# Sixteen interleaved groups of eight rows: another row order in the DRAM copy of streamed weights

## The chip, the cores and the metric

The kernel runs on one core of one Trainium2 chip. The metric is the time of one execution on the device in microseconds (us), as the median of several runs. An execution counts as slow when it is over 1.5% above the fastest of the same kernel, and ratios use fast executions only. Below, before and after name the kernel without and with the change.

The engines have short names in the profiles: PE does the matmuls (PEld its weight loads), DVE, ACT and POOL (also called GpSimd) the work on vectors, and SP here only issues DMA transfers. SBUF is the on-chip memory; the kernel's tiles there have 128 partitions, and each row of a weight chunk goes to one of them.

## The reference

The reference computes two independent things and puts them side by side. Part A is a long convolution by FFT. Part B is a recurrent attention over 64 segments of 32 tokens, in which each segment's memory is the output of the one before, so the segments run one after another:

```python
def _B_ref(x, mem0, Wq, Wk, Wv, Wo, seg_len):
    ...                                   # S = 2048, Dm = 1024, H = 32, Dh = 128, M = 8
    mem = mem0
    for s in range(n_seg):                # 64 segments
        xs = x[:, s * seg_len:(s + 1) * seg_len, :].copy()
        h = jnp.concatenate([mem, xs], axis=1)
        q = jnp.einsum('btd,dhe->bhte', h, Wq)      # k and v in the same way
        ...                               # masked softmax attention
        o = jnp.einsum('bhte,hed->btd', o, Wo)
        mem = o[:, :M, :].copy()
        outs.append(o[:, M:, :])
    ...
```

The four weight matrices of part B take 32 MB in bf16, and every segment needs all of them.

## The kernel before

The weights are cut into 64 chunks of 128 rows by 2048 bf16 columns (512 KB, 4 KB a row). Of these 43 stay in SBUF for good. The other 21 are streamed: before the loop they are copied into a DRAM tensor `WS`, one contiguous 512 KB block for each, and in every segment they are loaded again into a ring of six buffers. (One of them is kept aside after the first segment, which leaves 20 loads a segment and 1281 in all.)

```python
PITCH = 2048
...
    def stream_src(ch):
        return WS[ring_order.index(ch), :, 0:2048]
...
    WS = dram.tile([len(ring_order), 128, PITCH], BF, name="WS")
    for ch in ring_order:
        if ch[0] == 3:                                   # chunks of Wo: DRAM to DRAM
            nc.gpsimd.dma_start(dst_view(stream_src(ch), ch), dram_chunk(ch))
...
                    nc.sync.dma_start(t[:], dram_chunk(ch))          # chunks of Wq, Wk, Wv pass
                    if ch in streamed:                               # through SBUF (tile pw)
                        nc.gpsimd.dma_start(stream_src(ch), t[:])
...
    ring = ctx.enter_context(tc.tile_pool(name="b_ring", bufs=RING))  # RING = 6
    def fetch():
        if loads:
            s, ch = loads.pop(0)
            live[s, ch] = t = ring.tile([128, 2048], BF, tag="wring", name="wring")
            nc.sync.dma_start(t[:], stream_src(ch))                   # the load of this study
...
    def done(ch):                        # called after the last matmul that reads the chunk
        if ch in streamed:
            del live[now[0], ch]
            if now[0] == 0 or ch != order_s[KEPT_SLOT]:
                fetch()
```

## Time and profile before

| | before |
|---|---|
| median time | 2397.64 us (2394.31 to 2403.53, 3 runs) |
| first ring load issued | 568 us after the span's start |
| from the first ring packet to the last | 1819 us |
| DMA share and rate in the loop | 0.99, 381 GB/s |

The page of the profiled execution of before. The rows named PEclk, DMA and GB/s divide the span into 40 equal slices; in the first two a digit is a share in tenths (9 is 90% or more), the third is the rate. The last line is a DMA queue: packets, MB, share of the time of 16 engines.

```profile
span 2404.6 us, 76750 instructions
PE 1773.3 (74%) x33620; PEld 893.8 (37%) x33620; DVE 753.8 (31%) x2331; ACT 639.8 (27%) x1143; POOL 367.0 (15%) x1019
...
PEclk8899669996899999999989999999999999989999
DMA  7886985659999999999999999999999999999997
GB/s 280 305 283 206 376 275 140 183 156 387 401 357 393 370 394 369 400 365 399 380 383 379 375 400 376 393 369 402 384 383 375 388 371 397 375 396 385 388 384 288
...
q1 hardware_dynamic: 278120, 767.72, 84.1%
```

From about the tenth slice on the DMA engines are full and nothing else is. The same for the loop alone, in the table by stretches (the last three numbers of its row are granted PE clock, DMA share, GB/s):

```profile
core 0: us, PE busy (x) PEld busy (x) DVE busy (x) ACT busy (x) POOL busy (x), PEclk, DMA share, GB/s
571.00:2404.00 1833.00, 1439.97 (x32000) 748.53 (x32000) 498.40 (x1872) 435.45 (x833) 267.71 (x889) 0.93 0.99 381
```

A share of 0.99 with PE busy for 1440 of 1833 us means that the 16 DMA engines set the pace. The chain of work that ended last, as shares of the span, says the same: the ring load is its largest part.

```profile
DMA 55%; PE 28%; issue 6%; DVE 6%; ACT 2%; POOL 1%; SPq 0%; ACTq 0%; POOLq 0%; DVEq 0%
DMA wring<-WS 47%; PE acc L708 9%; PE yacc L796 5%; PE kb_ps L541 5%; PE tail_acc L657 3%; PE vb_ps L554 2%; DMA X_sb<-in_B_x_dram 1%; DMA SK<-s_sb 1%; DMA pw<-in_B_Wv_dram 1%; ACT s_sb L234 1%; DMA Wearly<-in_B_Wk_dram 1%; PE tps L723 1%; 
```

The costliest group, PE on streamed chunks (busy us, mean ns of one, then idle time before it and what ended it), PE's own waits for the ring (total us, times, longest us), and the line of the ring loads among the DMA issues (count, size, median us from issue to landing):

```profile
L708 PE MATMUL acc<-wring,rec 128*32 128x512 bf16 x4096 | 419.4, 414 | 166.0 <-DMA wring<-WS 131.9
```

```profile
PE acc L708 <- DMA wring<-WS: 131.9, 234, 2.6
...
PE yacc L796 <- DMA wring<-WS: 46.4, 129, 1.7
PE tps L628 <- DMA wring<-WS: 42.2, 3, 41.2
```

```profile
wring<-WS SPq DMA_DIRECT2D x1281, 512.0 KB, 7.3
```

PE waits little for the ring, only 132 + 46 + 42 us, although the DMA sets the pace: six loads run ahead.

One more reading comes from the trace's records of single DMA packets. A ring load moves as 128 packets of 4 KB, as many as it has rows, and 1281 loads make 163,968 of them. They take 161 ns in the median, 168 ns in the mean (160 and 169 over all 4 KB packets of that queue). There are 4-byte packets as well. The SP queue (q1) has 24,524, and 1527 x 16 + 6 x 15 + 2 x 1 = 24,524: 16 for each load, except for six of 15 rows and two of one row. I read this number as that of the DMA engines that take part in a load. The trace does not name a packet's engine, so this is a reading; it fits that 16 is also the number of ring packets under way for the largest part of the time (49%).

### The profile page before, as it was taken

The numbers are of one execution on the slowest core, as the hardware profiler recorded it, in microseconds if no ns is written. First come the engines' busy times: TensorE is split into PE (matmuls) and PEld (weight loads), VectorE is DVE, ScalarE is ACT, GpSimd is POOL, SyncE is SP. The second block draws the span as 40 slices with busy tenths as digits, with TensorE's granted clock in tenths as the row PEclk, the third lists the DMA queues.
The fourth block names the chain that finished last, engine by engine and source line by source line (L and its number), as shares of the span: only waits on it lengthen the run. The fifth ranks groups of instructions, "written<-read, shape, count | busy, mean of one in ns | idle before, by whom it ended". The sixth has DMA issues, their size and how long they took to land.

```text
span 2404.6 us, 76750 instructions
## 1 busy us (share of the span) xinstructions
PE 1773.3 (74%) x33620; PEld 893.8 (37%) x33620; DVE 753.8 (31%) x2331; ACT 639.8 (27%) x1143; POOL 367.0 (15%) x1019
## 2 busy tenths in 40 slices
PE   2655359773777787777877878787777778787776
PEld 1221134331333434343444434343434343444433
DVE  5978322111222222322222222322222223222222
ACT  6966011111222222222222222222222222222222
POOL 5034100000111111111111111111111111111111
PEclk8899669996899999999989999999999999989999
DMA  7886985659999999999999999999999999999997
GB/s 280 305 283 206 376 275 140 183 156 387 401 357 393 370 394 369 400 365 399 380 383 379 375 400 376 393 369 402 384 383 375 388 371 397 375 396 385 388 384 288
DMA packets 308617, 842.07 MB, mean 350 GB/s; under 512 B 83676, under 2 KB 91900, under 8 KB 308279
## 3 DMA queue, kind: packets, MB, share of 16 engines
q1 hardware_dynamic: 278120, 767.72, 84.1%
q0 software_dynamic: 20048, 45.76, 5.6%
q10 hardware_dynamic: 10112, 23.68, 3.0%
q8 instruction: 263, 4.31, 0.7%
q14 instruction: 74, 0.61, 0.1%
HBM read 777.14 MB, written 62.39 MB: 349 GB/s over the span
## 4 chain that ended last, share of the span: by engine, by line
DMA 55%; PE 28%; issue 6%; DVE 6%; ACT 2%; POOL 1%; SPq 0%; ACTq 0%; POOLq 0%; DVEq 0%
DMA wring<-WS 47%; PE acc L708 9%; PE yacc L796 5%; PE kb_ps L541 5%; PE tail_acc L657 3%; PE vb_ps L554 2%; DMA X_sb<-in_B_x_dram 1%; DMA SK<-s_sb 1%; DMA pw<-in_B_Wv_dram 1%; ACT s_sb L234 1%; DMA Wearly<-in_B_Wk_dram 1%; PE tps L723 1%; DMA Wlate<-in_B_Wo_dram 1%; POOL Yre L344 1%; DVE wring L592 1%
## 5 line engine op out<-in xcount | busy, mean ns | idle before, releaser
L708 PE MATMUL acc<-wring,rec 128*32 128x512 bf16 x4096 | 419.4, 414 | 166.0 <-DMA wring<-WS 131.9
L708 PEld LDWEIGHTS <-rec 128*32 128x32 bf16 x12288 | 325.2, 100 | 529.7 <-issue 273.1
L717 ACT CAST qkv_sb<-acc 128x512 bf16<-128x512 f32 x384 | 225.1, 586 | 823.8 <-PE acc L708 775.4
L708 PE MATMUL acc<-Wearly,rec 128*32 128x512 bf16 x4608 | 385.7, 428 | 4.7 <-DVE YB L669 4.7
L796 PEld LDWEIGHTS <-OT 128*32 128x32 bf16 x8192 | 228.4, 101 | 206.0 <-issue 145.3
L796 PE MATMUL yacc<-Wlate,OT 128*32 128x256 bf16 x5632 | 257.4, 290 | 55.3 <-issue 55.2
L708 PE MATMUL acc<-Wlate,rec 128*32 128x512 bf16 x3584 | 276.4, 380 | 0.0
L796 PE MATMUL yacc<-wring,OT 128*32 128x256 bf16 x2560 | 143.8, 288 | 69.2 <-DMA wring<-WS 46.4
L815 DVE COPY KT<-tps 128x512 bf16<-128x512 bf16 x64 | 27.2, 425 | 398.4 <-PE tps L723 398.4
L685 POOL COPY KT<-rec 128x128 bf16<-128x128 bf16 x128 | 38.8, 303 | 664.3 <-DVE wring L592 519.1
L629 DVE COPY rec<-tps 128x64 bf16<-128x64 bf16 x64 | 12.3, 192 | 373.3 <-PE tps L628 363.9
L864 POOL DMA_DIRECT2D out_dram<-Y x64 | 46.0, 719 | 509.0 <-ACT Y L859 484.0
L782 ACT CAST OT<-OTp 128x512 bf16<-128x512 f32 x128 | 75.0, 586 | 164.4 <-PE OTp L773 161.1
L859 ACT CAST Y<-yacc 128x256 bf16<-128x256 f32 x64 | 23.8, 372 | 299.9 <-PE yacc L796 299.9
L723 PE MATMUL tps<-ident,qkv_sb 128*128 128x128 bf16 x1024 | 101.2, 221 | 1.9 <-DVE tps L592 1.9
L723 PEld LDWEIGHTS <-qkv_sb 128*128 128x128 bf16 x1024 | 58.8, 97 | 112.0 <-issue 84.9
L622 POOL DMA_DIRECT2D rec<-REC x64 | 37.4, 584 | 385.7 <-issue 181.7
L786 DVE CAST OTB<-OTp 128x128 bf16<-128x128 f32 x128 | 34.7, 271 | 182.8 <-ACT OT L782 182.8
L592 DVE TENSOR_SCALAR wring<-OTp 128x768 int32<-128x768 int32 x63 | 60.3, 958 | 93.7 <-PE acc L708 53.1
L692 POOL COPY QBm<-rec 128x32 bf16<-128x32 bf16 x512 | 84.6, 213 | 0.0
L541 PE MATMUL kb_ps<-XBT,Wearly 128*128 128x512 bf16 x288 | 81.8, 384 | 0.0
L818 DVE COPY QT<-tps 128x512 bf16<-128x512 bf16 x64 | 27.2, 425 | 160.5 <-PE tps L723 160.5
(201 smaller groups left out, 2233.6 us busy)
## 6 DMA issues: line engine op xcount, KB each, us to landing
wring<-WS SPq DMA_DIRECT2D x1281, 512.0 KB, 7.3
rec<-REC POOLq DMA_DIRECT2D x64, 192.0 KB, 6.3
SK<-s_sb SPq DMA_DIRECT2D x16, 512.0 KB, 4.8
SU<-s_sb SPq DMA_DIRECT2D x16, 512.0 KB, 3.6
Kg<-SK ACTq DMA_DIRECT2D x32, 256.0 KB, 4.2
Ug<-SU SPq DMA_DIRECT2D x32, 256.0 KB, 4.6
WS<-pw POOLq DMA_DIRECT2D x16, 512.0 KB, 6.8
REC<-stage SPq DMA_DIRECT2D x4, 2048.0 KB, 13.0
```

Of the source, the lines that this page charges most:

```text
L541: nc.tensor.matmul(ps[:], lhsT=ws[kc][:, hl * 128:(hl + 1) * 128], rhs=XBT[:, kc].rearrange("p s t -> p (s t)"), start=(kc == 0), stop=(kc ...
L554: nc.tensor.matmul(ps[:], lhsT=XBT[:, kc, 16 * tb:16 * tb + 16, :].rearrange("p s t -> p (s t)"), rhs=ws[kc][:, c * 512:(c + 1) * 512], st ...
L592: nc.vector.tensor_scalar(out=dst, in0=src, scalar1=0, scalar2=None, op0=ALU.bitwise_or)
L657: nc.tensor.matmul(self.acc[32 * dq:32 * dq + 32, 0:256], lhsT=self.OTB[:, c, 4 * g + i, :], rhs=w[:, o:o + 256], start=first, stop=not se ...
L685: nc.gpsimd.tensor_copy(KT[:, :, :, 32:40], KBs[:, 128 * g:128 * g + 128].rearrange("p (c i t) -> p i c t", c=4, i=4))
L692: nc.gpsimd.tensor_copy(q[:, :, 40 * i:40 * i + 8], QBs[:, 128 * g:128 * g + 128].rearrange("p (c i t) -> p c i t", c=4, i=4)[:, :, i, :])
L708: nc.tensor.matmul(self.acc[32 * c:32 * c + 32, :], lhsT=hT[:, kc, :], rhs=w[:, c * 512:(c + 1) * 512], start=(kc == 0), stop=(kc == 7), t ...
L717: nc.scalar.copy(sb[:], self.acc[:])
L723: nc.tensor.transpose(tp[:, i * 128:(i + 1) * 128], sb[:, i * 128:(i + 1) * 128], ident[:])
L782: nc.scalar.copy(OT[:], o_view(g)[:, :, :, 0:32])
L796: nc.tensor.matmul(yacc[32 * dq:32 * dq + 32, 0:256], lhsT=OT[:, c, i, :], rhs=w[:, hh * 1024 + dq * 256:hh * 1024 + (dq + 1) * 256], star ...
L864: nc.gpsimd.dma_start(bass.AP(outb.tensor, outb.offset + SEG * s * 2048, [[256, 4], [2048, 32], [1, 256]]), Y[:])
```

## The change

The rows of each chunk in `WS` are stored in another order: row `16 hi + lo` of the chunk goes to place `8 lo + hi`, with `hi` from 0 to 7 and `lo` from 0 to 15. The load reads them back through the same view, so the tile in SBUF, and every instruction after it, is as before. The likely intent was to have the DMA engines read neighbouring rows of the memory at the same moment instead of rows far apart.

```diff
     def stream_src(ch):
-        return WS[ring_order.index(ch), :, 0:2048]
+        return WS[ring_order.index(ch), :, 0:2048].rearrange("(lo hi) c -> hi lo c", hi=8)
...
     for ch in ring_order:
         if ch[0] == 3:
-            nc.gpsimd.dma_start(dst_view(stream_src(ch), ch), dram_chunk(ch))
+            for hh in range(2):
+                nc.gpsimd.dma_start(stream_src(ch)[:, :, hh * 1024:(hh + 1) * 1024],
+                                    dram_chunk(ch)[:, hh, :].rearrange("(hi lo) d -> hi lo d", hi=8))
```

In the built program the ring load has the same count, bytes and place as before. Only its DRAM side is now a pattern of two levels, 8 groups of 16 rows; below this is written [8][16], and the one of before [128].

## The prediction

> **What bounds the kernel now.** From 571 us to the end the kernel is a loop of 64 segments, about 28.6 us each, bound by the DMA engines: the table by stretches gives it a DMA share of 0.99 at 381 GB/s, PE busy 1440 of 1833 us. The largest entry of the chain of waits is DMA wring<-WS, 47%. The DMA issues list 1281 such loads of 512 KB, 20 a segment, or 164,000 packets of 4 KB. In the trace one takes 160 ns (median; mean 169), so the ring alone fills 1281 x 8 x 169 ns = 1730 us on each of 16 engines; the loop's other traffic is about 90 us per engine.
>
> **What the change does.** Bytes, packets and arithmetic stay; the permutation is written and undone consistently. In the built program the loop's one difference is the shape of the load: its DRAM side is [8][16] rows of 4 KB instead of [128], against 128 SBUF partitions. The copies into WS (five become ten halves, sixteen keep their size) get the same shape, in the first 571 us and mostly off the critical path: 0 to 20 us.
>
> **Why this matters.** [...] the SP queue's 24,524 of them are exactly 1527 loads x 16 + six 15-row loads x 15 + two one-row loads; the ACT queue's 1088 are 66 x 16 + four 8-row loads x 8. None of its DMAs shows it for [8][16].
>
> **Cost.** On 8 engines a load puts 16 packets on each: 1281 x 16 x 160 to 169 ns = 3280 to 3460 us, plus 90, plus 571: 3940 to 4120 us, all on the critical path. It may be worse. [...] The trace hints at such a cost: around 48.5 to 52 us, where 112-row loads run, 2 KB packets take about 128 ns, against 84 in 128-row loads. So I go above the clean sum.
>
> **Prediction.** 4300 us, 80% range 3850 to 5700. Faster by over 2%: 0.03; within 2%: 0.07; slower by over 2%: 0.90.
>
> **What would show each step.** (1) Half the engines: the SP queue's packets fall by 8 x 1281 = 10,248, from 278,120 to about 267,870; the loop's DMA share falls to about 0.5, its rate to about 200 GB/s or less. (2) Clean halving: 4 KB packets stay at 160 to 170 ns[...]. (3) PE's waits for wring<-WS grow from under 300 us to well over 1500. (4) The time before the loop stays within 30 us of 571. (5) Issue to landing of a ring load, 7.3 us now, at least doubles.
>
> **What would make it wrong.** If [8][16] still goes over all 16 engines (the packet count stays), the time stays near 2400 us[...]. If reading rows 32 KB apart eased or hurt the memory side, packets would leave 160 ns; I expect nothing there, since rows stay 4 KB contiguous.

What is marked as cut are reasons that no trace of this case shows: in the third paragraph the ground on which I took 8 engines from the outer dimension of 8, in the others the grounds for slower packets and their cost. "Of them" means 4-byte packets and "it" a load's number of engines. The 8 stands as an assumption; in the trace of before only loads of fewer than 16 rows have fewer than 16 of these packets (8 for 8 rows, 15 for 15, 1 for 1). The sum on 8 engines is whole, 3280 to 3460 + 90 + 571 = 3940 to 4120 us. The addition of 180 us from its top to the 4300 predicted is not worked out.

## The result

| | before | after |
|---|---|---|
| median time | 2396.28 us (2394.31 to 2403.53, 4 runs) | 4019.23 us (4010.61 to 4032.57, 4 runs) |
| span of the profiled execution | 2404.6 us | 4030.8 us |
| first ring load issued | 568 us | 589 us |
| first ring packet to last | 1819 us | 3427 us |
| 4 KB ring packet, median and mean | 161 and 168 ns | 160 and 166 ns |
| 4-byte packets on the SP queue | 24,524 | 14,276 |

The ratio is 1.677, 95% interval 1.671 to 1.683. A ratio is the mean time of one kernel's fast runs over that of the other's of the same rounds, so it is not quite the ratio of the medians quoted here.

The page of after, the same lines as for before:

```profile
span 4030.8 us, 76732 instructions
PE 2373.8 (59%) x33598; PEld 1053.4 (26%) x33620; DVE 769.4 (19%) x2331; ACT 640.1 (16%) x1143; POOL 370.1 (9%) x1024
...
PEclk8877976666667676766666767666676666666666
DMA  7877665555555555555555555555555555555554
GB/s 252 294 254 256 161 234 209 208 210 206 207 205 204 204 204 208 203 201 206 204 208 208 207 203 206 206 197 206 201 203 204 187 201 196 200 206 207 205 204 171
...
q1 hardware_dynamic: 267872, 767.68, 49.7%
```

The loop in the table by stretches, the chain, the group, PE's waits, and the issues:

```profile
core 0: us, PE busy (x) PEld busy (x) DVE busy (x) ACT busy (x) POOL busy (x), PEclk, DMA share, GB/s
571.00:4030.00 3459.00, 2037.21 (x32000) 906.89 (x32000) 513.62 (x1872) 435.46 (x833) 266.93 (x889) 0.66 0.53 204
```

```profile
DMA 84%; PE 10%; issue 2%; DVE 1%; ACT 1%; POOL 1%; SPq 0%; ACTq 0%; POOLq 0%; DVEq 0%
DMA wring<-WS 78%; PE acc L710 4%; PE kb_ps L543 3%; PE vb_ps L556 1%; DMA X_sb<-in_B_x_dram 1%; PE yacc L798 1%; ACT s_sb L234 1%; DMA SK<-s_sb 1%; DMA Wlate<-in_B_Wo_dram 1%; DMA zt<-SZ 1%; POOL Yre L344 0%; DMA out_dram<-ot 0%; DMA Wearl
```

```profile
L710 PE MATMUL acc<-wring,rec 128*32 128x512 bf16 x4096 | 553.2, 527 | 1048.6 <-DMA wring<-WS 1046.8
```

```profile
PE acc L710 <- DMA wring<-WS: 1046.8, 876, 4.6
PE yacc L798 <- DMA wring<-WS: 267.3, 252, 4.0
...
PE tps L630 <- DMA wring<-WS: 42.1, 1, 42.1
```

```profile
wring<-WS SPq DMA_DIRECT2D x1281, 512.0 KB
```

The SP queue has lost 278,120 - 267,872 = 10,248 packets, which is 8 for each of the 1281 loads, and its 4-byte packets fell by the same 10,248. The bytes are the same. The mean share of the engines fell to 0.53, yet the loop takes nearly twice as long. A share of 0.53 that never moves fits half the engines at full load and half nearly idle, and so does the number of ring packets under way at once: 16 before and 8 after for the largest part of the time (table below). The page gives no landing time for the ring loads of after.

The difference of the spans, 1626 us, is 1608 us in the ring's time, 21.5 us ahead of it, and 3 us less behind the last packet. PE's matmuls on the ring grew from 414 to 527 ns, but PE does not set the pace here: the granted clock fell from 0.93 to 0.66 in the loop, in which PE waits for 1047 + 267 + 42 us on the ring. The clock was lower where PE was less busy: in the stretch from 700 to 2300 us PE is busy for 79, 60 and 36% of the time in before, after and the run with outer dimension 4 below, and the clock is 0.93, 0.67 and 0.51. So I read the slower matmuls as a consequence of waiting; no run tests that alone.

### The profile page after: what moved, and what is told of

Read it like the earlier page. It is cut to its first block, busy times and chain, and to the rows that moved or that the text cites. A ratio compares the mean times of both kernels' runs of the same rounds, so it can differ in the third digit from the quotient of the medians.

```text
span 4030.8 us, 76732 instructions
## 1 busy us (share of the span) xinstructions
PE 2373.8 (59%) x33598; PEld 1053.4 (26%) x33620; DVE 769.4 (19%) x2331; ACT 640.1 (16%) x1143; POOL 370.1 (9%) x1024
## 3 DMA queue, kind: packets, MB, share of 16 engines
q1 hardware_dynamic: 267872, 767.68, 49.7%
## 4 chain that ended last, share of the span: by engine, by line
DMA 84%; PE 10%; issue 2%; DVE 1%; ACT 1%; POOL 1%; SPq 0%; ACTq 0%; POOLq 0%; DVEq 0%
DMA wring<-WS 78%; PE acc L710 4%; PE kb_ps L543 3%; PE vb_ps L556 1%; DMA X_sb<-in_B_x_dram 1%; PE yacc L798 1%; ACT s_sb L234 1%; DMA SK<-s_sb 1%; DMA Wlate<-in_B_Wo_dram 1%; DMA zt<-SZ 1%; POOL Yre L344 0%; DMA out_dram<-ot 0%; DMA Wearly<-in_B_Wk_dram 0%; PE tps L725 0%; DMA Wlate<-in_B_Wv_dram 0%
## 5 line engine op out<-in xcount | busy, mean ns | idle before, releaser
L710 PE MATMUL acc<-wring,rec 128*32 128x512 bf16 x4096 | 553.2, 527 | 1048.6 <-DMA wring<-WS 1046.8
L710 PEld LDWEIGHTS <-rec 128*32 128x32 bf16 x12288 | 376.1, 115 | 1665.2 <-issue 1274.8
L710 PE MATMUL acc<-Wearly,rec 128*32 128x512 bf16 x4608 | 528.6, 561 | 2.1 <-DVE YB L671 0.9
L798 PEld LDWEIGHTS <-OT 128*32 128x32 bf16 x8192 | 299.8, 126 | 473.9 <-issue 337.6
L710 PE MATMUL acc<-Wlate,rec 128*32 128x512 bf16 x3584 | 392.4, 523 | 0.0
L798 PE MATMUL yacc<-wring,OT 128*32 128x256 bf16 x2560 | 181.5, 374 | 307.5 <-DMA wring<-WS 267.3
L798 PE MATMUL yacc<-Wlate,OT 128*32 128x256 bf16 x5632 | 343.6, 383 | 0.0
L725 PE MATMUL tps<-ident,qkv_sb 128*128 128x128 bf16 x1024 | 120.5, 252 | 3.2 <-DVE tps L594 3.2
L725 PEld LDWEIGHTS <-qkv_sb 128*128 128x128 bf16 x1024 | 69.7, 110 | 162.6 <-issue 127.4
L762 DVE STREAM_TRANSPOSE PT<-P_pad 128x128 bf16<-128x128 bf16 x256 | 73.7, 288 | 193.8 <-PE OTp L775 193.8
```

What stands on the lines that cost most here:

```text
L710: nc.tensor.matmul(self.acc[32 * c:32 * c + 32, :], lhsT=hT[:, kc, :], rhs=w[:, c * 512:(c + 1) * 512], start=(kc == 0), stop=(kc == 7), t ...
L725: nc.tensor.transpose(tp[:, i * 128:(i + 1) * 128], sb[:, i * 128:(i + 1) * 128], ident[:])
L762: nc.vector.transpose(out=PT[:, kb, :, 0:32], in_=P_pad[:, 0:4, ks])
L798: nc.tensor.matmul(yacc[32 * dq:32 * dq + 32, 0:256], lhsT=OT[:, c, i, :], rhs=w[:, hh * 1024 + dq * 256:hh * 1024 + (dq + 1) * 256], star ...
```

## The experiments

Three theories stood at the start. Theory 1: the outer dimension of 8 leaves only 8 of 16 engines. Theory 2: the memory serves rows in the new order more slowly. Theory 3: a two-level pattern is handled more slowly by the queue that issues it (one issue of the ring load takes 572 ns in after, 320 in before). The issues alone cannot be the limit in after: 1281 x 572 ns = 733 us, against 3427 us for the ring.

Passages marked as cut in the expectations are reasons that no run shows.

All numbers on packets below are counted from the trace's packet records, ring loads only, from the first ring packet on. "In flight" is the number of ring packets under way that holds for the largest part of that time. In the GpSimd run the 4 KB packets of its queue are counted, and 1.4% of them are not ring packets. The row of sixteen_outer is from a slow execution.

```
kernel             shape of load    mean ns  median ns  in flight (share of the time)
before             [128]              168      161      16 (49%)
after              [8][16]            166      160       8 (77%)
natural_eight      [8][16]            165      160       8 (77%)
four_outer         [4][32]            162      160       4 (89%)
sixteen_outer      [16][8]            255      259      16 (53%)
natural_sixteen    [16][8]            243      245      16 (53%)
one_level_spread   [128]              170      160      16 (49%)
every_other        [128], [8][16]     238      209       8 (33%), 16 (22%)
grouped_half       [128], [8][16]     195      161       8 (40%), 16 (18%)
two_halves         [64] + [64]        264      265      16 (50%)
low_half           [64]               313      325      16 (42%)
middle_half        [64]               199      159      16 (17%), none (16%)
middle_two_level   [16][4]            200      159      none (16%), 16 (15%)
gpsimd_queue       [8][16]            323      301      16 (40%)
```

### Outer dimension 16: the same idea on all engines

```diff
-        return WS[ring_order.index(ch), :, 0:2048].rearrange("(lo hi) c -> hi lo c", hi=8)
+        return WS[ring_order.index(ch), :, 0:2048].rearrange("(lo hi) c -> hi lo c", hi=16)
```

(and `hi=16` in the copies of Wo)

> The same kind of permutation, written with an outer dimension of 16: [16][8] rows in place of [8][16]; each row still lies apart from the next, now by 64 KB. Theory 1 (the outer dimension of 8 left only 8 of 16 DMA engines): all 16 engines again, the SP queue's packets back at 278,120, time within 2% of before, about 2400 us. Theory 2 (the memory is slower when rows are read out of order): still slow, 3500 us or more, with 4 KB packets well over 160 ns. Theory 3 (a two-level pattern is handled more slowly by the queue that issues it, 572 ns an issue against 320): still slow, near 4000 us, since this pattern has two levels as well.

Measured: 3239.85 us median of six runs (3177 to 3287), ratio 1.336 (1.329 to 1.342) from the fast runs. The profiled execution was a slow one, at 3265 us. No theory had this: Theory 1 had said about 2400 us, the other two 3500 us or more and near 4000 us. Its SP queue, from the page, and its row in the table by stretches from 700 to 2300 us (from here on always that stretch, with the columns as above: the last three are clock, DMA share, GB/s):

```profile
q1 hardware_dynamic: 278120, 767.72, 89.4%
```

```profile
700.00:2300.00 1600.00, 1031.60 (x19152) 484.98 (x19148) 304.38 (x1114) 259.15 (x497) 160.68 (x534) 0.80 1.02 260
```

All 278,120 packets are back, so all 16 engines take part. Their share is 1.02 in this stretch, but the rate is 260 GB/s, because a packet takes 255 ns instead of 168. (That is the slow execution; a fast one of the same shape, natural_sixteen below, has 243 ns.) So Theory 1 explains the count and is not the whole story of such patterns. Something makes packets slow here that did not make them slow in after. This became Theory P, below.

### Natural order, outer dimension 8

```diff
-        return WS[ring_order.index(ch), :, 0:2048].rearrange("(lo hi) c -> hi lo c", hi=8)
+        return WS[ring_order.index(ch), :, 0:16, :]
...
-    WS = dram.tile([len(ring_order), 128, PITCH], BF, name="WS")
+    WS = dram.tile([len(ring_order), 8, 17, PITCH], BF, name="WS")
```

> The other corner: rows in their natural order, but with a gap of one row after every 16, so that the load keeps the shape [8][16]. Theory 1: as slow as the change, 3950 to 4100 us, SP packets 267,872. Theory 2: about 2400 us, since the order is natural. Theory 3: about 4000 us.

Measured: 4009.66 us (3994.15 to 4026.53, 4 runs), ratio 1.671 (1.667 to 1.675), against 1.677 for the change. The rows lie in their natural order, with one unused row after every 16, and it is as slow as the change.

```profile
q1 hardware_dynamic: 267872, 767.68, 49.8%
```

```profile
700.00:2300.00 1600.00, 951.32 (x15094) 425.04 (x15090) 240.90 (x878) 203.63 (x391) 125.66 (x420) 0.67 0.53 206
```

So the new row order is not the cause; the outer dimension is. Theory 2 falls for the change itself.

### Outer dimension 4

The diff is that of the change, with `hi=4`.

> The permutation with an outer dimension of 4. Theory 1: 4 engines, SP packets 278,120 - 12 x 1281 = 262,748; 1281 x 32 packets x 160 to 167 ns = 6560 to 6850 us plus 100 plus 590: 7250 to 7540 us. Theories 2 and 3: about as the change, near 4000 us, since order and issue cost are alike. [...]

Measured: 7201.09 us, a single run of unknown state. The packets on the SP queue are exactly as counted in advance (the 4-byte packets among them are 9152, 4 for each ring load), and packets stay at 160 ns with 4 in flight:

```profile
q1 hardware_dynamic: 262748, 767.66, 27.2%
```

```profile
700.00:2300.00 1600.00, 580.11 (x7806) 244.74 (x7806) 122.34 (x446) 104.31 (x200) 66.08 (x219) 0.51 0.27 107
```

The ring ran from 626 to 7187 us, 6561 us, and 1281 x 32 x 160 ns = 6559 us. Halving the engines again nearly doubles the ring's time, from 3427 us. This also speaks against Theory 3: for 89% of the time exactly 4 ring packets are under way, each at its usual 160 ns, so I take it that 4 engines are busy without a pause and are not held up by the issuing queue. An issue took 4.8 us in the median here; why was not tested.

The time ahead of the loop differs with the shape of the writes into `WS`, which are the only other thing changed: the first ring load is issued at 568 us with [128], 572 to 573 with outer dimension 16, 587 to 589 with 8, and 624 with 4.

### The change on every other chunk

```diff
-        return WS[ring_order.index(ch), :, 0:2048].rearrange("(lo hi) c -> hi lo c", hi=8)
+        i = ring_order.index(ch)
+        w = WS[i, :, 0:2048]
+        return w.rearrange("(lo hi) c -> hi lo c", hi=8) if i % 2 else w
```

(the copies of Wo follow the same condition)

> The change on every other streamed chunk: 577 of the 1281 loads are [8][16], 704 stay [128]. Theory 1, if the 8-engine loads always take the same 8 engines: these carry 704 x 8 + 577 x 16 = 14,864 ring packets at 167 ns, 2480 us, plus 100 us of other traffic and about 580 us ahead of the loop: about 3160 us. Theory 1, if their 8 engines rotate: the load stays even, about 2450 us. SP packets in both cases 278,120 - 8 x 577 = 273,504.

Measured: 4032.92 us (4028.01 to 4042.11, 4 runs), ratio 1.681 (1.678 to 1.683). The packet count is exact, 273,504, but both times were missed: 45% of the change costs all of it.

```profile
q1 hardware_dynamic: 273504, 767.70, 68.1%
```

```profile
700.00:2300.00 1600.00, 922.79 (x14726) 418.69 (x14722) 238.29 (x870) 201.15 (x386) 122.00 (x410) 0.66 0.74 201
```

The share, 0.74, is far above the 0.53 of after, yet the rate is about the same, 201 GB/s against 206 in that stretch: packets take longer, 238 ns in the mean and 209 in the median. So loads of the two shapes disturb each other. The run also tells which engines the [8][16] loads use. If these are the same 8 each time, the 8 carry 14,864 ring packets, at 238 ns 3540 us, and the ring took 3438 us; spread evenly over 16 engines it would have been 2440 us. So on the SP queue it is the same 8 each time, as far as this estimate from the mean packet goes.

### Theory P and its tests

The slow packets of [16][8] and of the mixture called for a theory. Theory P: it matters which SBUF partitions the engines write at the same moment; where their writes meet, each is slowed, and a packet takes longer. I called the place where they meet a port, hence the P; no trace shows one. Which partitions meet in which load I took from reasons that this case does not show; they are left out, and the figures that the expectations below give for Theory P, such as 250 to 320 ns, stand as guesses. Its rival, Theory M: rows read 64 KB apart (or in some other order) are slow in memory when 16 engines ask. Two runs separate them.

**Natural order, shape [16][8].**

```diff
-        return WS[ring_order.index(ch), :, 0:2048].rearrange("(lo hi) c -> hi lo c", hi=8)
+        return WS[ring_order.index(ch), :, 0:8, :]
...
-    WS = dram.tile([len(ring_order), 128, PITCH], BF, name="WS")
+    WS = dram.tile([len(ring_order), 16, 9, PITCH], BF, name="WS")
```

(an edit to after, with `hi=16` in the copies of Wo)

> Rows in natural order with a gap of one row after every 8, so that the load has the shape [16][8] of the sixteen_outer run, which used all 16 engines but had 4 KB packets of 255 ns. Theory P[...]: as sixteen_outer, 3150 to 3300 us, packets about 255 ns. Theory M (the memory serves rows that lie apart more slowly): near before, 2400 to 2450 us, packets 160 to 170 ns.

Measured: one fast run at 3152 us, three slow at 3209 to 3249 us, against 2400 us for before. The row of the fast run, which was the profiled one:

```profile
700.00:2300.00 1600.00, 1068.59 (x20006) 504.80 (x20009) 318.65 (x1170) 271.58 (x521) 168.71 (x561) 0.80 1.02 273
```

**One level, rows 64 KB apart** (edit to the kernel before).

```diff
-        return WS[ring_order.index(ch), :, 0:2048]
+        i = ring_order.index(ch)
+        return WS[i // 16, :, i % 16, 0:2048]
...
-    WS = dram.tile([len(ring_order), 128, PITCH], BF, name="WS")
+    WS = dram.tile([2, 128, 16, PITCH], BF, name="WS")
```

> The kernel before with its one-level load [128], but the copy laid out so that the rows of a chunk lie 64 KB apart. Theory P: near before, 2380 to 2450 us, packets 160 to 170 ns. Theory M: about 3200 us, packets about 255 ns.

Measured: 2418.31 us (2415.12 to 2421.30, 4 runs), ratio 1.008 (1.005 to 1.011).

```profile
700.00:2300.00 1600.00, 1256.77 (x27920) 650.44 (x27916) 434.78 (x1635) 378.20 (x725) 232.84 (x775) 0.93 1.00 380
```

Natural order in the wrong shape is slow (243 ns); spread rows in the right shape are fast (160 ns in the median). Spreading rows costs 0.8%, so Theory M is not the cause. This does not yet show Theory P; the next runs bear on it.

**Two halves of 64 partitions** (edit to the kernel before).

```diff
-            nc.sync.dma_start(t[:], stream_src(ch))
+            for h in range(2):
+                nc.sync.dma_start(t[64 * h:64 * h + 64, :], stream_src(ch)[64 * h:64 * h + 64, :])
```

> The kernel before, each ring load split into two, partitions 0 to 63 and 64 to 127; every load on 16 engines, rows in order. Theory P[...] packets take 250 to 320 ns and the time is 3150 to 4000 us. Without a port limit: packets stay 160 to 170 ns, the second issue costs SP only, and the time is within 3% of before.

Measured: 3378.48 us (3346.89 to 3403.24, 4 runs, one of them slow), ratio 1.404 (1.396 to 1.412). There is no second level and the row order is untouched, and packets still take 264 ns. This is what Theory P expected. By itself it could also be a cost of small or doubled loads. The half loads below rule out the size; the doubled number was not tested alone, but 16 packets stay in flight for the largest part of the time (50%), and the DMA share is 1.03, so the engines do not wait for loads.

```profile
700.00:2300.00 1600.00, 1038.06 (x18658) 436.90 (x18662) 295.68 (x1084) 251.54 (x483) 156.58 (x519) 0.77 1.03 254
```

**The change on the second half of a segment's chunks.** The diff is that of every_other, with `i >= len(ring_order) // 2` in place of `i % 2`.

> The change on half the chunks as in the every_other run, but on the second ten loads of a segment, where that run alternated. If its slow packets (238 ns mean) come from [8][16] loads running side by side with [128] loads[...], they should now be rare outside the two borders of a segment: 15,376 packets[...] at about 170 to 190 ns, 3250 to 3600 us. If any mixture costs as much: 4050 to 4200 us. If the mixture's cost has nothing to do with neighbours in time, the same 4050 to 4200 us.

Measured: 3510.24 us (3500.54 to 3519.57, 4 runs), ratio 1.463 (1.457 to 1.468). The 15,376 packets of the expectation are 640 x 8 + 641 x 16, what each of 8 engines carries if the [8][16] loads always take the same 8. There are more [8][16] loads than in every_other (641 against 577), and it is 520 us faster.

```profile
700.00:2300.00 1600.00, 999.87 (x17545) 488.08 (x17547) 279.87 (x1025) 237.44 (x455) 148.11 (x491) 0.71 0.73 239
```

The median packet is back at 161 ns and the mean at 195. So the cost of the mixture depends on loads of unlike shape being neighbours in time. This fits Theory P, but the run shows the disturbance and not its place.

**Half loads on chosen partitions.** The next three give a wrong result. They are the kernel before, with the six ring buffers allocated once; the first six ring loads are whole, all later ones bring 64 of the 128 rows:

```diff
-            nc.sync.dma_start(t[:], stream_src(ch))
+            if full[0] > 0:
+                full[0] -= 1
+                nc.sync.dma_start(t[:], stream_src(ch))
+            else:
+                nc.sync.dma_start(t[0:64, :], stream_src(ch)[0:64])      # low_half
+              # nc.sync.dma_start(t[32:96, :], stream_src(ch)[0:64])     # middle_half
+              # nc.sync.dma_start(t[32:96, :], stream_src(ch).rearrange(
+              #     "(a b) c -> a b c", b=8)[:, 0:4, :])                 # middle_two_level
```

> Wrong result on purpose: after the first six ring loads each load brings only half its rows, one level [64], into partitions 0 to 63. Theory P[...], packets 250 to 320 ns. Theory 3 (a two-level pattern is what slows a packet): one level, so packets 160 to 170 ns.

> Wrong result on purpose: as low_half, same bytes and same rows, but into partitions 32 to 95[...]. Theory P:[...] packets 160 to 175 ns. If the low half's slowness comes from loads of 64 partitions as such: as low_half, 250 ns or more.

> Wrong result on purpose: as middle_half, but the load's DRAM side has two levels, [16][4] with gaps. Theory P:[...] packets 160 to 175 ns in spite of the two levels. Theory 3: about 250 ns, as in the two runs of shape [16][8].

Measured, one run of unknown state each: 2608.13, 2216.89 and 2227.78 us. From the pages of low_half, middle_half and middle_two_level, in this order, the span, the SP queue and the ring loads among the issues:

```profile
span 2606.4 us, 76357 instructions
...
q1 hardware_dynamic: 196520, 433.49, 73.8%
...
wring<-WS SPq DMA_DIRECT2D x1275, 256.0 KB, 6.5
```

```profile
span 2215.0 us, 76357 instructions
...
q1 hardware_dynamic: 196520, 433.49, 59.9%
...
wring<-WS SPq DMA_DIRECT2D x1275, 256.0 KB, 4.2
```

```profile
span 2226.0 us, 76357 instructions
...
q1 hardware_dynamic: 196520, 433.49, 59.8%
...
wring<-WS SPq DMA_DIRECT2D x1275, 256.0 KB, 4.2
```

The packets and bytes are the same to the last one, and so are the 4-byte packets, 24,524 as in before, which makes 16 engines a load in all three; but the engines' time for packets is 73.8% of the span on partitions 0 to 63 and 59.9% on 32 to 95. The median packet is 325 ns, twice the 159 ns of the other. (An estimate from this: 16 packets of 4 KB in 325 ns are 202 GB/s, no more than the 205 GB/s of 8 packets in 160 ns.) With two levels on partitions 32 to 95 it is again 159 ns. So among these half loads the partitions reached decide, and neither the levels nor the number of partitions do; Theory 3 falls here a second time. The mean of the two fast ones, 199 and 200 ns, is over the 175 that I had allowed. These kernels leave the DMA idle for 16% of the time, so their loads come in bursts, and a tenth of their packets take over 300 ns; that tail was not studied.

### The ring from the GpSimd queue

```diff
-            nc.sync.dma_start(t[:], stream_src(ch))        # in fetch(), of the change
+            nc.gpsimd.dma_start(t[:], stream_src(ch))
```

> The change, bytes and shape kept, with the ring loads issued from the GpSimd queue[...]. Theory 1 with rotation: both halves of the engines share the loads, more than 8 ring packets in flight, faster than the change: 2450 us if nothing collides, up to 3400 us if packets collide[...] as in the [16][8] runs. If GpSimd also uses the same 8 engines each time: 4000 us or more. GpSimd's own waits may add to either.

Measured: 4115.81 us (4081.46 to 4152.06, 4 runs, one slow), ratio 1.711 (1.697 to 1.725). That the engines rotate on this queue was my assumption. The trace fits it: in each of the four copies into `WS` that run alone in this trace, in the [8][16] shape and from the same queue (issued at 396 to 480 us), at most 8 packets are in flight, while the ring has 16 for the largest part of the time (40%) and more than 8 for 97% of it. But a packet takes 323 ns in the mean, and the rate is that of 8 engines again:

```profile
q0 software_dynamic: 371248, 718.12, 89.2%
```

```profile
700.00:2300.00 1600.00, 873.65 (x14504) 412.64 (x14508) 231.57 (x854) 198.04 (x380) 457.99 (x992) 0.70 1.04 198
```

The 3400 us that I had given as the worst case was too low: two [8][16] loads side by side, on two sets of 8 engines, seem to slow each other by as much as the second set adds (198 GB/s from 700 to 2300 us, against 206 in after). Why is not shown, also because the queue differs: it has 144 packets of 4 bytes for each ring load where the SP queue has 8, so counting them does not give the number of engines here.

## Why the prediction was right

**The mechanism and the size.** The time, 4019 us, lies in the "clean halving" of the prediction, 3940 to 4120 us; the 4300 us named as the most likely was 7% too high. The SP queue's packets came out at 267,872 (predicted about 267,870), the loop's share at 0.53 (0.5), its rate at 204 GB/s (200), the packet at 160 ns. The assumption of 8 engines for an outer dimension of 8 held for this two-level pattern (8 ring packets in flight for 77% of the time), and the 2x2 of order and outer dimension shows what decides: [128] 2400 us and [8][16] 4010 us in natural order, [8][16] 4019 us in the new one. The fourth corner, the new kind of order on 16 engines, was not clean (3240 us), as its shape alone costs about as much (3152 us in natural order); but rows spread in memory at [128] cost only 0.8%.

**What did not come.** I went from the clean sum up to 4300 us for packets slowed by collisions. In after there are none to speak of: packets take 160 ns. The term of the sum that was mis-sized is this addition, 180 us over the top of the clean sum; it measured as nothing. Which partitions a load reaches did matter in the half loads (325 ns in low_half against 159 in middle_half), and it was right to look for slow packets. But where all loads had the same two-level shape on the SP queue, they came with 16 engines at work (243 to 255 ns) and not with 8 or 4 (160 ns). The hint that I took from the 112-row loads (128 ns against 84) was not tested by any run; it does not carry over to 8 engines. Why 8 engines escape is not shown. Nor is which partitions each engine writes in a two-level load: the trace does not name a packet's engine.

**Smaller points.** The time ahead of the loop grew by 21.5 us, just over the 0 to 20 us I gave. PE's waits for the ring grew from 220 to 1356 us, short of "well over 1500": the loop's PE busy time grew by 597 us at the lower clock, which probably took up part of the waiting. The landing time could not be read, since the page of after has none for the ring.

## What to carry to other kernels

Before a DRAM tensor's layout is rearranged, look at the outermost dimension that the load's pattern then has: an outer 8 or 4 against 128 partitions left 8 or 4 ring packets in flight here instead of 16, and in this DMA-bound loop the ring's time went from 1819 us to 3427 and 6561. Count the SP queue's 4-byte packets, or its packets at equal bytes, to see how many engines a load uses (16, 8 and 4 a load in these runs; on the GpSimd queue the count did not tell); a DMA share that sits near one half (0.53 here) while everything waits for DMA points the same way. An outer 16 was not enough either: a load of one level over all 128 partitions ran at 160 ns a packet, while the same bytes as [16][8], or as two halves of 64 partitions, took 243 to 264 ns.
